# Seven products for eight in part of the first layer, with sums on GpSimd and copies on ScalarE

## The chip, the cores and the metric

The kernel runs on one core of a Trainium2 chip, with one launch. The metric is the device time of that core in microseconds (us), lower is better. Three runs of the kernel before took 331.85, 331.86 and 332.35 us; the median is 331.86 us. A separate execution was profiled, and its trace is what the views below are taken from. Its stated TensorE clock is 1.000 of full speed.

## The reference, cut to what matters

```python
B, H, S, Nb, D = 8, 8, 576, 16, 64           # q, k, v: B x H x S x D; beacon_k, beacon_v: B x H x Nb x D
scores = q @ concat(beacon_k, k).T / sqrt(D) # causal over k; the 16 beacon keys are seen by every query
a = softmax(scores)
x = (a @ concat(beacon_v, v)).transpose(0, 2, 1, 3).reshape(4608, 512)
h = x @ w_in                                 # first layer, 512 -> 2048
g = h * sigmoid(1.702 * h)
out = g @ w_out                              # second layer, 2048 -> 512, float32
```

So an attention over 8 batches is followed by two dense layers over 4608 tokens. All matrix products run on fp16 operands and add up in fp32.

## The kernel before, in words

**Attention.** The work is cut into 16 sets, a set being one batch and four of its heads. A set's scores are computed transposed (keys on the partitions) by `e_qk` (L458) in chunks of at most 512 columns for four heads, exponentiated by ScalarE in `e_exp` (L469), and masked by GpSimd in `e_mask` (L490). VectorE adds the key blocks of a set in `e_zadd` (L508). `e_av` (L545) forms the values and, with a matrix of ones, the row sums. VectorE turns and inverts the row sums (`e_z1`, `e_z2`) and writes the normalised values to `xT` (L580, `e_norm`). GpSimd also issues the loads of q, k, v and of the weights.

**The dense layers.** Tokens are taken in ten groups: two of 256 and eight of 512 (groups 2 to 9). The first layer of a group is 16 tiles of 128 hidden units each (`e_m1`, L604): four matmuls of 512 columns add up in one PSUM bank, and ScalarE applies the gate in `e_gelu` (L625) from PSUM to the fp16 tile `g`. The second layer of groups 2 to 9 is already done by Strassen's scheme in Winograd's form: `g` and `w_out` are cut into two by two blocks, VectorE makes four sums of blocks of `g` (`e_s`, L669), and TensorE does seven products instead of eight (`e_prod`, L718, 16 matmuls of 256 columns each). ScalarE copies the first product out of PSUM (`e_half`, L729), VectorE joins the others to it (`e_join`, L734), and SP stores the four quarters (`e_store4`, L741).

**PSUM.** The scores hold four banks. The four others form a ring (`RING`, `ring_tile`), shared by the tiles of the first layer, the values, and the products of the second layer. A ring bank is free again when its closing instructions (a gate, a norm, a join) are done.

**Order.** The order is written out beforehand: `Plan.run` takes operations with planned durations and dependences, and gives each engine a fixed sequence, which is then emitted. `choose` picks TensorE's next operation. `QUOTAS` says after how many chunks of scores a group's first layer may start, and when it has started (`inside`), its 16 tiles go before other dense work, and no scores are started. `T_ATT0` and `T_ATT1` spread the due times of the attention's loads and transposes. Each engine executes its sequence in order, so an instruction that waits holds up all that is behind it on its engine.

```python
        m1, m2 = first(("m1",)), first(("m2",))
        if m1 and inside:
            return m1
        if m1 and m2:
            return m2 if last == "m1" or free["ACT"] > t + 1500 else m1
```

TensorE's matmuls have three forms here: scores use row groups of 32, values use column groups of 32, and the dense layers use the whole array. In the order before, the form changes 145 times. After the last values, TensorE has the first layers of groups 8 and 9 and the products of groups 7, 8 and 9 left.

Of the kernel before, what the change touches and what calls it, by code (L numbers as in the profile page):

```python
# [13 lines left out]
NEAR = 500  # L14
IDLE = 800
# [9 lines left out]
class Plan:  # L25
# [5 lines left out]
    def __init__(self, ring):  # L31
        self.ops = []
        self.bank = [None] * ring
        self.tiles = {}
        self.closers = {}
        self.quota = {}
# [18 lines left out]
    def ring_free(self):  # L55
        best = None
        for i, key in enumerate(self.bank):
            t = 0
            for c in self.closers[key] if key is not None else ():
                t = None if t is None or c.start is None else max(t, c.end + 60)  # L60
            if t is not None and (best is None or t < best[0]):
                best = (t, i)
        return best

    def run(self):
# [8 lines left out]
        group, inside, ntile, nchunk = min(self.quota), False, 0, 0  # L74
        firsts = {}
        for o in self.ops:
            if o.kind == "m1":
                firsts.setdefault(o.pr, o)

# [5 lines left out]
        def allowed(o):  # L85
            if o.kind == "m2" and o.ring not in self.tiles:
                if sum(left_of[k] > 0 for k in self.tiles if k in left_of) >= 2:
                    return False
            if o.kind == "m1":
                return o.pr < group or (o.pr == group and (inside or group not in self.quota))  # L90
            if o.kind == "qk":
                return not inside
            if o.table is not None and o.table != table:
                return due_of_table[table] == 0
            return True
# [3 lines left out]
        while todo:  # L99
# [4 lines left out]
            slot = self.ring_free()  # L104
            ringt = slot[0] if slot else None
            for e, cand in avail.items():
                t = None
                for o in cand:
                    if not allowed(o):
                        continue  # L110
                    r = max(o.ready, o.due)
                    if o.ring is not None and o.ring not in self.tiles:
                        if ringt is None:
                            continue
                        r = max(r, ringt)
                    if t is None or r < t:
                        t = r
                if t is not None:
                    t = max(t, free[e])
                    if best is None or t < best[0]:  # L120
                        best = (t, e)
# [8 lines left out]
            for o in avail[e]:  # L130
# [3 lines left out]
                if o.ring is not None and o.ring not in self.tiles:  # L134
                    if ringt is None:
                        continue
                    r = max(r, ringt)
                if r <= t:
                    ok.append(o)
            if e == "PE":  # L140
                o = self.choose(ok, t, mode, last, free, inside)
# [8 lines left out]
            if e == "PE":  # L150
# [3 lines left out]
                if o.ring is not None and o.ring not in self.tiles:  # L154
                    self.tiles[o.ring] = slot[1]
                    self.bank[slot[1]] = o.ring
            if o.kind == "m1":
                ntile += 1 if o.pr == group else 0
                if inside and ntile == 16:
                    group, inside, ntile = group + 1, False, 0  # L160
# [30 lines left out]
    def choose(self, ok, t, mode, last, free, inside):  # L191
# [15 lines left out]
        late = first(("av",), lambda o: o.ready + 7000 <= t)  # L207
# [11 lines left out]
def kernel(  # L219
# [42 lines left out]
    pss = ctx.enter_context(tc.tile_pool(name="pss", bufs=1, space=bass.MemoryType.PSUM))  # L262
    psu = ctx.enter_context(tc.tile_pool(name="psu", bufs=1, space=bass.MemoryType.PSUM))

# [6 lines left out]
    QUOTAS = (19, 28, 38, 42, 48, 55, 55, 55)  # L271
    HM, HN = 256, NNT // 2
    xT = cst.tile([P, NKT, XR], F16, tag="xT", name="xT")
# [84 lines left out]
    plan = Plan(RING)  # L358

    def ring_tile(key):  # L360
        if key not in rings:
            i = plan.tiles[key]
            rings[key] = psu.tile([P, 512], F32, tag=f"u{i}", name=f"u{i}")
# [228 lines left out]

    def e_m1(g, n0, n1):
        t0, t1 = GROUPS[g]
        w = t1 - t0
        if g not in gts:
            gts[g] = gp.tile([P, NNT, 512], F16, tag="g", name="g")
# [90 lines left out]

    def quarter(g, i, j):
# [35 lines left out]

    def e_half(g, p, dst):
# [19 lines left out]
    T_ATT0, T_ATT1 = 17000, 249000  # L746
# [109 lines left out]

    def two_back(s, half):
# [3 lines left out]
    def values(s):  # L861
# [7 lines left out]
        for i in range(1, NJ if whole else 0):  # L869
# [3 lines left out]
                op("DVE", 75 + 0.517 * 4 * w, deps + sums[-1:], lambda i=i: e_zadd(s, i), pr=3, name="zadd")  # L873
            )
        for n, (x, half) in enumerate(order):
# [20 lines left out]
            if x == 2:  # L896
                z1 = op(
                    "DVE", 65 + 1.045 * cols, [avs[(s, x, half)]], lambda h=half: e_z1(s, h), pr=0, closes=key, name="z1"
# [4 lines left out]
                )  # L903
            else:
# [43 lines left out]
    SQ, SDVE, TDUE = 2, 0, 60000  # L948
# [9 lines left out]
    def products(g):  # L958
        eng = "POOL" if g < SDVE else "DVE"
        sd = {}  # L960
        for n0 in range(0, HN, SQ):
            n1 = n0 + SQ
            prev = []
            for i in range(4):
                deps = prev + done.get(g - 1, [])
                for n in range(n0, n1):
                    deps += [gates[(g, n)], gates[(g, n + HN)]]
# [8 lines left out]
        def prod(p):  # L976
            prev = []
            for n0 in range(0, HN, SQ):
# [3 lines left out]
                else:  # L982
                    deps += [gates[(g, n + (HN if p in (2, 4) else 0))] for n in range(n0, n0 + SQ)]
# [34 lines left out]
        store(c22, "u", 1, 1)  # L1018
        prod(3)
        c12 = join(3, "m", "m", [u4])  # L1020
        store(c12, "m", 0, 1)
        ends[g] = c12

    def mlp(g):
# [16 lines left out]
        for n0 in firsts:  # L1041
            n1 = n0 + n
            key = ("m1", g, n0)
# [56 lines left out]
    for o in done.get(NPL - 1, []) + done.get(NPL - 2, []) if tds else ():  # L1100
        also(tds[3], o)
    plan.quota.update(zip(range(GEL, NG), QUOTAS))
# [32 lines left out]
```

## Time and profile before

| | before |
|---|---|
| median of three runs | 331.86 us |
| profiled execution, its own time | 331.71 us |
| span of the profiled execution | 330.0 us |
| TensorE busy | 311.5 us |
| VectorE busy | 237.5 us |
| ScalarE busy | 203.6 us |
| GpSimd busy | 116.9 us |
| TensorE's first matmul starts at | 8.22 us |
| TensorE's last matmul ends at | 326.17 us |

The profiled execution is the time of one run; its span goes from the first to the last instruction, and 1.71 us of the run lie outside the span. Busy times count each instruction from its start to its end. Since TensorE works on several matmuls at once, the mean duration of one matmul in a group's row is longer than the step from one to the next; the step is read from the starts in the timeline. A line number in a view is a line of the kernel; "out<-in" gives the tiles written and read.

### The profile page before, as it was taken

The numbers are of one execution on the slowest core, as the hardware profiler recorded it, in microseconds if no ns is written. First come the engines' busy times: TensorE is split into PE (matmuls) and PEld (weight loads), VectorE is DVE, ScalarE is ACT, GpSimd is POOL, SyncE is SP. The second block draws the span as 40 slices with busy tenths as digits, with TensorE's granted clock in tenths as the row PEclk, the third lists the DMA queues.
The fourth block names the chain that finished last, engine by engine and source line by source line (L and its number), as shares of the span: only waits on it lengthen the run. The fifth ranks groups of instructions, "written<-read, shape, count | busy, mean of one in ns | idle before, by whom it ended". The sixth has DMA issues, their size and how long they took to land. (4 is left out here: it accounts for less than half of the span.)

```text
span 330.0 us, 9837 instructions
## 1 busy us (share of the span) xinstructions
PE 311.5 (94%) x4288; PEld 210.9 (64%) x4288; DVE 237.5 (72%) x478; ACT 203.6 (62%) x234; POOL 116.9 (35%) x178
## 2 busy tenths in 40 slices
PE   0699899999999999999999999999999999999995
PEld 0477666545885467646878877447774664746884
DVE  4847959796998788987999589978896630460484
ACT  1676487787767786777758586858677427175000
POOL 8765557572238205360427046702422000000000
PEclk9999999999999999999999999999999999999999
DMA  7999999569017903392149623930120000110122
GB/s 126 161 205 208 200 178 156 83 105 130 29 41 140 145 2 82 89 129 50 47 95 127 85 53 89 127 85 2 34 96 3 2 32 2 46 51 2 66 96 95
DMA packets 58219, 28.81 MB, mean 87 GB/s; under 512 B 41280, under 2 KB 53568, under 8 KB 58176
## 3 DMA queue, kind: packets, MB, share of 16 engines
q0 software_dynamic: 47552, 18.49, 47.7%
q1 hardware_dynamic: 10560, 9.69, 8.9%
q8 instruction: 33, 0.54, 0.7%
q14 instruction: 10, 0.08, 0.1%
q10 hardware_dynamic: 64, 0.01, 0.0%
HBM read 37.22 MB, written 9.44 MB: 141 GB/s over the span
## 5 line engine op out<-in xcount | busy, mean ns | idle before, releaser
L604 PE MATMUL u<-xT,w 128*128 128x512 f16 (+1 forms) x704 | 130.7, 343 | 2.1 <-DVE g L637 1.1
L469 ACT ACTIVATE E<-s 128x2048 f16<-128x2048 f32 (+4 forms) x66 | 98.8, 1514 | 42.7 <-PE s L458 42.0
L604 PEld LDWEIGHTS <-w 128*128 128x128 f16 x704 | 68.0, 98 | 58.5 <-issue 3.2
L625 ACT ACTIVATE g<-u 128x512 f16<-128x512 f32 x128 | 74.4, 598 | 43.2 <-PE u L604 43.0
L490 POOL TENSOR_SCALAR_AFFINE_SELECT E<-E 128x512 f16<-128x512 f16 (+3 forms) x78 | 52.0, 689 | 119.9 <-ACT E L469 116.2
L734 DVE SCALAR_TENSOR_TENSOR osb<-u,osb 128x512 f32<-128x512 f32 x56 | 37.4, 680 | 40.5 <-PE u L718 26.9
L718 PEld LDWEIGHTS <-g 128*128 128x128 f16 x512 | 48.6, 98 | 7.3 <-issue 0.2
L458 PE MATMUL s<-qT,kT 32*128 32x32 f16 (+20 forms) x1376 | 35.9, 235 | 11.7 <-DVE qT L429 10.3
L718 PE MATMUL u<-w,g 128*128 128x256 f16 x384 | 46.0, 273 | 0.0
L458 PEld LDWEIGHTS <-kT 32*128 32x128 f16 x1376 | 26.0, 95 | 29.1 <-issue 14.7
L718 PEld LDWEIGHTS <-sA 128*128 128x128 f16 x384 | 36.4, 98 | 4.9
L718 PE MATMUL u<-tB,sA 128*128 128x256 f16 x256 | 31.3, 273 | 0.0
L389 POOL DMA_DIRECT2D vb<-in_v_dram x32 | 27.3, 866 | 2.5 <-DMA kn<-in_k_dram 1.5
L545 PE MATMUL u<-E,vb 128*32 128x352 f16 (+8 forms) x928 | 27.7, 267 | 0.0
L580 DVE TENSOR_TENSOR xT<-u,rz 128x352 f16<-128x352 f32 (+2 forms) x52 | 24.9, 518 | 1.7 <-PE u L545 1.1
L508 DVE TENSOR_TENSOR zs<-zs,E 128x1344 f16<-128x1344 f16 (+2 forms) x36 | 23.5, 652 | 3.1 <-POOL E L490 0.5
L545 PEld LDWEIGHTS <-vb 128*32 128x32 f16 (+1 forms) x928 | 20.1, 98 | 5.4 <-issue 1.3
L429 DVE STREAM_TRANSPOSE kT<-kn 128x576 f32<-128x576 f32 x16 | 20.1, 1258 | 4.4 <-PE s L458 2.8
L669 DVE TENSOR_TENSOR sA<-g 128x512 f16<-128x512 f16 x32 | 12.8, 417 | 12.2 <-ACT g L625 11.9
L429 DVE STREAM_TRANSPOSE qT<-qn 128x576 f32<-128x576 f32 x16 | 20.0, 1249 | 2.2 <-PE s L458 1.8
L557 DVE STREAM_TRANSPOSE zt<-u 128x352 f32<-128x352 f32 (+2 forms) x32 | 13.8, 459 | 9.0 <-PE u L545 8.9
L718 PE MATMUL u<-tB,g 128*128 128x256 f16 x128 | 16.3, 273 | 0.0
(44 smaller groups left out, 229.1 us busy)
## 6 DMA issues: line engine op xcount, KB each, us to landing
out_dram<-osb SPq DMA_DIRECT2D x36, 256.0 KB, 2.2
kn<-in_k_dram POOLq DMA_DIRECT2D x16, 288.0 KB, 5.6
qn<-in_q_dram POOLq DMA_DIRECT2D x16, 288.0 KB, 6.3
vb<-in_v_dram POOLq DMA_DIRECT2D x24, 128.0 KB, 5.2
w<-in_moe_w_in_dram POOLq DMA_DIRECT2D x8, 256.0 KB, 9.2
w<-in_moe_w_out_dram POOLq DMA_DIRECT2D x4, 512.0 KB, 14.0
vb<-in_v_dram POOLq DMA_DIRECT2D x8, 112.0 KB, 3.7
vb<-in_v_dram POOLq DMA_DIRECT2D x8, 80.0 KB, 5.0
```

What stands on the lines that cost most here:

```text
L389: nc.gpsimd.dma_start(out=t[0 : hi - lo, j, h0:h1, :], in_=v[b, h0:h1, lo:hi, :].rearrange("h n d -> n h d"),)
L429: nc.vector.transpose(out=f32(dst.rearrange("p n e -> p (n e)")).rearrange("p (r t) -> p t r", t=TR), in_=f32(src[:, :]).rearrange("p (t c ...
L458: nc.tensor.matmul(sc[:, h, o : o + w], kT[s % NB2][r : r + 32, j * P : (j + 1) * P, d], qT[s % NB2][r : r + 32, a : a + w, d], start=(d = ...
L469: nc.scalar.activation(out=Es[s][:, :, c0:c1], in_=ss[i][:, :, o : o + c1 - c0], func=AFT.Exp, scale=0.125,)
L490: nc.gpsimd.affine_select(out=blk, in_=blk, compare_op=ALU.is_ge, fill=0.0, base=off + (Nb if j == 0 else 0), pattern=[[0, Q], [1, w]], ch ...
L508: nc.vector.tensor_tensor(out=t, in0=E[:, :, Z0:S] if i == 1 else t, in1=E[:, :, wcol[i] : wcol[i] + S - a], op=ALU.add,)
L545: nc.tensor.matmul(u[32 * h : 32 * h + 32, a:e], lhs, src[0:kw, h, col : col + e - a], start=first, stop=last,)
L580: nc.vector.tensor_tensor(out=xT[:, 2 * hs + x : 2 * hs + x + n, t0 : t0 + w], in0=rings[("av", s, x, half)][:, 0 : n * w].rearrange("p (n ...
L604: nc.tensor.matmul(u[:, o + a - t0 : o + e - t0], w1t[:, kp, nt * P : (nt + 1) * P], xT[:, kp, a % XR : (e - 1) % XR + 1], start=(kp == 0) ...
L625: nc.scalar.activation(out=gts[g][:, n0:n1, 0:w], in_=rings[("m1", g, n0)][:, 0 : n * w].rearrange("p (n w) -> p n w", n=n), func=AFT.Gelu ...
L718: nc.tensor.matmul(u[:, HM * mt : HM * (mt + 1)], lhs[:, n, mt * P : (mt + 1) * P], rhs[:, n, :], start=(n == 0 and mt == 0), stop=(n == H ...
L734: nc.vector.scalar_tensor_tensor(out=osbs[(g, dst)][:, :], in0=rings[("p", g, p)][:, :], scalar=scale_of(g), in1=osbs[(g, src)][:, :], op0 ...
```

## The change

The change works on the first layer of the last two groups. The 16 tiles of a group are four "quarters" of four tiles (two adjoining tiles and the two that stand eight further on). In two quarters of group 8 and three of group 9 the four tiles of 512 tokens are computed by Strassen's scheme instead of directly: `e_first` does seven products, each of four matmuls of 256 columns, in a PSUM bank of its own. VectorE makes four sums of blocks of `w_in` once (`e_wsum`) and four sums of blocks of `xT` per group (`e_xsum`). Products 1, 2, 3, 4 and 5 are copied from PSUM to SBUF in float32 by ScalarE (`e_fcopy`), products 6, 7 and 5 are added to such a copy by VectorE (`e_fjoin`), the four final sums are made by GpSimd in SBUF (`e_fadd`, float32, 128 x 512), and ScalarE's gate then reads SBUF (`e_fgelu`). These intermediates lie in the buffers of the attention's `E`, which are free by then.

The four PSUM banks of the scores become a second ring for these products once the last exponential is done. From group 8 on (`MIX`), tiles of the first layer no longer go before the products of the second layer. The last product of the last group is done for its two halves of rows in two banks, each with its own join and its own store, the second store from ScalarE's queue. Further, the constants of the plan are others (`NEAR`, `IDLE`, `QUOTAS`, `T_ATT0`, `T_ATT1`, `TDUE`, the planned time of `e_zadd`, the time after which values are preferred), so the order of the attention changes too. In the order after, TensorE's form changes 138 times.

```diff
--- before.py
+++ after.py
-NEAR = 500
-IDLE = 800
+NEAR = 680
+IDLE = 3300
+MIX = 8
+LATE1 = 0
...
-    def ring_free(self):
+    def ring_free(self, late):
         best = None
-        for i, key in enumerate(self.bank):
-            t = 0
+        if late and self.gate.start is None:
+            return None
+        for i in range(self.ring, self.ring + 4) if late else range(self.ring):
+            key = self.bank[i]
...
             if o.kind == "m1":
+                if group >= MIX:
+                    return True
                 return o.pr < group or (o.pr == group and (inside or group not in self.quota))
...
-                o = self.choose(ok, t, mode, last, free, inside)
+                o = self.choose(ok, t, mode, last, free, inside and (group < MIX or LATE1))
...
-        late = first(("av",), lambda o: o.ready + 7000 <= t)
+        late = first(("av",), lambda o: o.ready + 24000 <= t)
...
-    QUOTAS = (19, 28, 38, 42, 48, 55, 55, 55)
+    QUOTAS = (20, 28, 43, 46, 49, 55, 55, 55)
     HM, HN = 256, NNT // 2
+    FIRST = {7: (), 8: (1, 3, ), 9: (0, 1, 2, )}
+    FADD = 1150
...
     def ring_tile(key):
         if key not in rings:
             i = plan.tiles[key]
-            rings[key] = psu.tile([P, 512], F32, tag=f"u{i}", name=f"u{i}")
+            if i >= RING and not late_s:
+                scores.close()
+                late_s.append(ctx.enter_context(tc.tile_pool(name="psl", bufs=1, space=bass.MemoryType.PSUM)))
+            rings[key] = (psu if i < RING else late_s[0]).tile([P, 512], F32, tag=f"u{i}", name=f"u{i}")
         return rings[key]
...
+    def wsum(i):
+        t = late_tile(0)[:, 2048 * i : 2048 * (i + 1)] if i < 3 else late_tile(1)[:, 0:2048]
+        return t.rearrange("p (k n) -> p k n", k=2)
...
+    def e_wsum(i):
+        s1, s2, s4, s3 = (wsum(x) for x in range(4))
+        if i == 0:
+            add("DVE", s1, wq(1, 0), wq(1, 1), ALU.add)
...
+    def e_first(g, d, p):
+        u = ring_tile(("n", g, d, p))
+        lhs, rhs = {
+            1: (wq(0, 0), xq(g, 0, 0)),
+            2: (wq(0, 1), xq(g, 1, 0)),
+            3: (wsum(2), xq(g, 1, 1)),
+            4: (wq(1, 1), xsum(g, 2)),
+            5: (wsum(0), xsum(g, 0)),
+            6: (wsum(1), xsum(g, 1)),
+            7: (wsum(3), xsum(g, 3)),
+        }[p]
+        for t in range(2):
+            n = (2 * d + t) * P
+            for k in range(2):
+                nc.tensor.matmul(
+                    u[:, HM * t : HM * (t + 1)],
+                    lhs[:, k, n : n + P],
+                    rhs[:, k, :],
+                    start=(t == 0 and k == 0),
+                    stop=(t == 1 and k == 1),
+                )
+
+    def e_fcopy(g, d, p, dst):
+        nc.scalar.copy(out=part(d, dst), in_=rings[("n", g, d, p)][:, :])
+
+    def e_fjoin(g, d, p, src, dst):
+        nc.vector.tensor_tensor(
+            out=part(d, dst), in0=rings[("n", g, d, p)][:, :], in1=part(d, src), op=ALU.add
+        )
+
+    def e_fadd(d, src, dst):
+        nc.gpsimd.tensor_tensor(out=part(d, dst), in0=part(d, dst), in1=part(d, src), op=ALU.add)
+
+    def e_fgelu(g, d, x, i, j):
+        n0 = 2 * d + HN * i
+        nc.scalar.activation(
+            out=group_tile(g)[:, n0 : n0 + 2, HM * j : HM * (j + 1)],
+            in_=part(d, x).rearrange("p (t w) -> p t w", t=2),
+            func=AFT.Gelu_apprx_sigmoid,
+        )
 
...
+    def e_prod_last(g, mt):
+        u = ring_tile(("p", g, 3, mt))
+        for n in range(HN):
+            nc.tensor.matmul(
+                u[:, 0:HM],
+                sA[2][:, n, mt * P : (mt + 1) * P],
+                w2t[:, HN + n, HM:],
+                start=(n == 0),
+                stop=(n == HN - 1),
+            )
+
+    def e_join_last(g, mt):
+        t = osbs[(g, "m")][:, HM * mt : HM * (mt + 1)]
+        nc.vector.scalar_tensor_tensor(
+            out=t, in0=rings[("p", g, 3, mt)][:, 0:HM], scalar=scale_of(g), in1=t, op0=ALU.mult, op1=ALU.add
+        )
+
+    def e_store_last(g, mt):
+        t0 = GROUPS[g][0] + mt * P
+        (nc.scalar if mt else nc.sync).dma_start(
+            out=out[t0 : t0 + P, HM:], in_=osbs[(g, "m")][:, HM * mt : HM * (mt + 1)]
+        )
...
-    T_ATT0, T_ATT1 = 17000, 249000
+    T_ATT0, T_ATT1 = -1000, 245000
...
-                op("DVE", 75 + 0.517 * 4 * w, deps + sums[-1:], lambda i=i: e_zadd(s, i), pr=3, name="zadd")
+                op("DVE", 75 + 0.6 * 4 * w, deps + sums[-1:], lambda i=i: e_zadd(s, i), pr=3, name="zadd")
...
-    SQ, SDVE, TDUE = 2, 0, 60000
+    SQ, SDVE, TDUE = 2, 0, 75000
...
+        if g == NG - 1:
+            for mt in range(2):
+                o = op(
+                    "PE", HN * 109, [sd[(2, n0)] for n0 in range(0, HN, SQ)] + [last[5]],
+                    lambda mt=mt: e_prod_last(g, mt), kind="m2", pr=g,
+                    ring=("p", g, 3, mt), mode="m", name=f"m2.{g}.3.{mt}",
+                )
+                o = op(
+                    "DVE", 335, [o, u4], lambda mt=mt: e_join_last(g, mt), pr=2, closes=("p", g, 3, mt), name="join"
+                )
+                op("ACT" if mt else "SP", 60, [o], lambda mt=mt: e_store_last(g, mt), name="store")
+            return
...
+    def first_quarters(g, d, xs, old):
+        if not wsums:
+            for i in range(4):
+                wsums.append(op("DVE", 1130, wsums[-1:], lambda i=i: e_wsum(i), pr=3, name="wsum"))
+            needs.append((wsums[0], NSET - 3))
+            needs.append((wsums[3], NSET - 2))
+        if (g, 0) not in xsums:
+            deps = list(xs)
+            deps += [o for o in m1s.get(g - 1, []) if o.ring[0] == "n"]
+            for i in range(4):
+                xsums[(g, i)] = o = op("DVE", 336, deps, lambda i=i: e_xsum(g, i), pr=2, name="xsum")
+                deps = [o]
+            needs.append((xsums[(g, 0)], NSET - 2))
...
+        def prod(p):
+            deps = xs + old + [w for n in (2 * d, 2 * d + 1, 2 * d + HN) for w in w1_of[n]]
+            deps += [wsums[lhs[p]]] if lhs[p] is not None else []
+            deps += [xsums[(g, rhs[p])]] if rhs[p] is not None else []
+            last[p] = op(
+                "PE", 4 * 109, deps, lambda: e_first(g, d, p), kind="m1", pr=g,
+                ring=("n", g, d, p), mode="m", name=f"m1.{g}.{d}.{p}",
+            )
+            m1s.setdefault(g, []).append(last[p])
+
+        def buf(x):
+            return x.upper() if x in "uv" and d % 2 else x
+
+        def reads(x, o):
+            readers.setdefault(buf(x), []).append(o)
+
+        def writes(x):
+            return readers.pop(buf(x), [])
+
+        def copy(p, dst, closes=True):
+            o = op(
+                "ACT", 480, [last[p]] + writes(dst), lambda: e_fcopy(g, d, p, dst), pr=1,
+                closes=("n", g, d, p), name="fcopy",
+            )
+            needs.append((o, NSET - 1))
+            return o
+
+        def join(p, src, dst, deps):
+            return op(
+                "DVE", 605, [last[p]] + deps + (writes(dst) if src != dst else []),
+                lambda: e_fjoin(g, d, p, src, dst), pr=2, closes=("n", g, d, p), name="fjoin",
+            )
+
+        def final(src, dst, deps, i, j):
+            o = op("POOL", FADD, deps, lambda: e_fadd(d, src, dst), pr=3, name="fadd")
+            reads(src, o)
+            e = op("ACT", 520, [o] + old, lambda: e_fgelu(g, d, dst, i, j), pr=1, name="fgelu", table="g")
+            reads(dst, e)
+            for n in (2 * d + HN * i, 2 * d + HN * i + 1):
+                gates.setdefault((g, n), {})[j] = e
+
+        prod(1)
+        m = copy(1, "m")
+        prod(2)
+        final("m", "a", [m, copy(2, "a")], 0, 0)
+        prod(6)
+        u2 = join(6, "m", "v", [m])
+        reads("m", u2)
+        prod(7)
+        u3 = join(7, "v", "u", [u2])
+        prod(4)
+        final("u", "b", [u3, copy(4, "b")], 1, 0)
+        prod(5)
+        final("u", "c", [u3, copy(5, "c")], 1, 1)
+        u4 = join(5, "v", "v", [u3])
+        prod(3)
+        final("v", "a", [u4, copy(3, "a")], 0, 1)
...
+            if n0 % HN // SQ in FIRST.get(g, ()):
+                if n0 < HN and n0 % SQ == 0:
+                    first_quarters(g, n0 // SQ, xs, old)
+                continue
...
+    for o, s in needs:
+        for (t, x, h), d in avs.items():
+            if t == s:
+                also(o, d)
+        also(o, qks[CH_OF[NSET - 1][0]])
```

## The prediction

> **What bounds the kernel now.** I read the page's busy shares, its slices and the chain that ended last, then a table of stretches, then timelines for the step of each kind of work.
>
> ```profile
> PE 311.5 (94%) x4288; PEld 210.9 (64%) x4288; DVE 237.5 (72%) x478; ACT 203.6 (62%) x234; POOL 116.9 (35%) x178
> PE   0699899999999999999999999999999999999995
> PE u L604 16%; PE u L718 15%; PE u L545 2%; PE s L458 1%; DVE zs L508 1%; ACT E L469 1%; DVE osb L734 0%; ACT L625 0%; DVE xT L580 0%; ACT g L625 0%; DVEq L508 0%
> ```
>
> TensorE (PE) is idle for 18.5 us: 8.2 before its first matmul, 3.8 after its last, 2.1 at 9 us, and ten gaps of 0.1 to 1.1 us that add up to 4.3. The chain's end is dense matmuls alone. So work taken off PE counts one for one, unless it brings waits. In the table of stretches the second covers the time from the end of the last values to PE's end (columns: length, then PE, PEld, DVE, ACT, POOL busy):
>
> ```profile
> 17.60:267.80 250.20, 246.54 (x3724) 166.09 (x3713) 202.56 (x398) 176.72 (x194) 102.71 (x152) 1.00 0.64 93
> 267.80:326.20 58.40, 58.37 (x416) 39.84 (x408) 23.31 (x52) 20.30 (x34) 0.00 (x0) 1.00 0.12 42
> 326.20:330.00 3.80, 0.00 (x0) 0.00 (x0) 0.69 (x1) 0.00 (x0) 0.00 (x0) 1.00 0.39 138
> ```
>
> There PE is full, ScalarE a third busy, VectorE 40%, GpSimd idle: room for what the change adds. The timeline gives the steps (start, length, what):
>
> ```profile
> 287.74 13.98 PE L604 MATMUL u<-xT,w 128*128 128x512 f16 x64
> ...
> 301.55 3.66 PE L718 MATMUL u<-w,g 128*128 128x256 f16 x32
> ...
> 324.26 1.91 PE L718 MATMUL u<-w,sA 128*128 128x256 f16 x16
> ...
> 326.21 0.69 DVE L734 SCALAR_TENSOR_TENSOR osb<-u,osb 128x512 f32<-128x512 f32 x1 [0.46 <-PE u L718]
> ```
>
> From 287.74 to 301.55, 64 matmuls of 512 columns: 0.2158 us each. From 301.55 to 326.17, 224 of 256 columns: 24.44 us and 0.18 of pipeline, 0.1091 each.
>
> [...]
>
> ```profile
> 198.89 0.64 POOL L490 TENSOR_SCALAR_AFFINE_SELECT E<-E 128x512 f16<-128x512 f16 x1 [1.83 <-ACT E L469]
> 201.72 3.74 POOL L490 TENSOR_SCALAR_AFFINE_SELECT E<-E 128x512 f16<-128x512 f16 x4 [2.19 <-ACT E L469]
> ```
>
> Alone a mask takes 0.64. Four take at most 2.56, but 3.74 while VectorE ran two sums of two SBUF tensors (1.12 and 1.10 us): 1.2 us more for 2.2 of overlap, 0.55 per us.
>
> **The change part by part, against the profiled 331.71 (span 330.0 and 1.71 around).**
>
> *First layer.* Five quarters lose 5 x 16 matmuls of 512: 80 x 0.2158 = 17.27. They gain 5 x 7 x 4 of 256: 140 x 0.1091 = 15.27. PE: **-2.0**.
>
> *Changes of form.* The order has 138 instead of 145. Their price:
>
> ```profile
> 85.97 1.92 PE L718 MATMUL u<-tB,sA 128*128 128x256 f16 x16
> 87.82 0.65 PE L458 MATMUL s<-qT,kT 32*128 32x336 f16 x24
> 88.40 1.61 PE L545 MATMUL u<-E,vb 128*32 128x224 f16 x56
> ```
>
> 16 steps are 1.745 but the next work starts after 1.85: 0.11. The scores stream 4096 columns on four row groups, [...] and take 0.58: 0.15. So 7 x 0.13 = **-0.9**; bounds -1.1 and -0.5[...].
>
> *The end.* The last join covers 256 columns instead of 512. VectorE's rows rise by about 1.04 ns per column (514 at 352, 615 at 448, line L580), so 0.69 becomes 0.42: -0.27. The last store carries 128 KB instead of 256 (2.2 us to landing) from ScalarE's queue, whose instructions are done; smaller transfers are unshown on this queue, so 0 to -0.3, I take -0.1. The first half's join and store end within the second half's 8 x 0.109 = 0.87 of matmuls or shortly after. **-0.4**.
>
> *ScalarE, VectorE, GpSimd in the last 50 us.* ScalarE gets 25 copies; 20 gates go and 20 come, reading SBUF (at the same 0.6, by the nearest row). VectorE gets 15 joins of 0.69, eight sums of `xT` at 0.42 and four sums of weights at 1.2. GpSimd gets 20 adds[...]. Beside the adds VectorE runs group 8's 16 sums (step 0.336: four take 1.42), four sums of `xT` and one of weights, 7.9 us of some 34[...] I take 1.3. In group 9 a quarter's seven products alternate with as many steps of the second layer: 14 x 4 x 0.109 = 6.1 us. In that time GpSimd has 4 x 1.3 = 5.2, ScalarE nine instructions of 0.6 - 0.09: 4.6. Both fit, and that cover holds while an add stays under 6.1 / 4 = 1.53.
>
> New waits: ScalarE works in order, so a gate that waits for an add holds the copies behind it, these hold PSUM banks, and a product needs the bank of the fourth one before it. Following the first quarter of group 8 from the last values: product 1 ends after 4.3 us, its copy at 5.15, product 4 needs that bank at 6.1; product 3 needs a bank that a join frees at 6.7, and starts at 6.9. Group 8's sums for tiles 6 and 7 come through the second quarter's last add: there the slack is some 0.5 us. Taken: **+0.6** (0 to +3). Set 15's values now follow its row sums after only six steps of a product. From the start of set 14's values PE needs 1.55 for these, 0.37 for the row sums and 24 x 0.109 = 2.62 for the product, so it is there after 4.5 us. VectorE starts on the row sums at about 2.1 and has two turns (0.53, 0.37), two reciprocals (0.16, 0.18), two expansions (0.41, 0.55) and a norm (0.51) to do, 2.7 less what neighbours overlap: 4.5 to 5.0 with the signal. **+0.3** (0 to +1).
>
> *Attention in another order.* The three early sums of weights (3.6 us) fall among set 14's sums, where VectorE is over 90% busy in several slices; the first-layer tiles of groups 3 to 6 run in one piece. GpSimd's loads and masks keep their number, and their due times move earlier; SP's stores are 32 + 4 before, 31 + 4 + 1 and one on ScalarE after. The trace cannot price the reordering: the gaps total 4.3 now, so at best about -2; at worst I allow +3, three waits as long as the longest (1.09). **0** taken: PE's content there is the same, with the same three starts of a first layer right after scores (0.3 each).
>
> Sum: -2.0 - 0.9 - 0.4 + 0.6 + 0.3 = -2.4: 329.3 for the profiled execution. The median of the runs stands 0.15 above the profiled time: **329.5**.
>
> **Rivals.** (1) *The gain is spent on new gaps in the attention*: VectorE, 72% busy, is late for values and norms by some 2.4 us in all. For it: the DVE slices full of 9s. Against it: only 3.6 us of work is added there, over many operations. Time 331.9. (2) *GpSimd becomes the bound of the last stretch, and it ends slower.* At d us per add, group 9's 12 adds cost 12 (d - 1.53), group 8's about 1 us more; with the 0.6 of waits counted above taken off, the gain of 2.4 is gone from d = 1.7. At 1.9 it costs 5.4 - 0.6 = 4.8: 334.3. [...] Against it: [...] joins from PSUM read one SBUF tensor. (3) *The reordering also removes gaps*, about 1.5 of the 4.3: 328.0. That the change doesn't do what it says is excluded: the counts stand in the order.
>
> **How the numbers follow.** A measurement of this kernel can tell about 0.2%, 0.7 us, from no change. My forecast has 0.60 and rival 3 0.12: faster. Rival 1 has 0.13, of it 0.09 within 0.2% and 0.04 slower; rival 2 has 0.15. So 0.72 faster, 0.09 same, 0.19 slower. The range leaves out one in ten on each side: from 327.3, rival 3 with a better tail, to 333.0, most of rival 1 and rival 2 up to about d = 1.8.
>
> **What would show it.** PE's busy time near 309, its last stretch full, its last matmul near 324; the adds' row at 1.1 to 1.5 us; ScalarE's waits for GpSimd short; the last join near 0.42. Rival 2 shows as adds over 1.7 and PE gaps that ScalarE's copies end after the last values; rival 1 as gaps before 250 us, released by VectorE. I am wrong if PE's work falls by less than 2.5 us.

## The result, and the profile after

The changed kernel takes 340.51 us (median of four runs, 339.76 to 341.33) where the kernel before takes 331.86: a ratio of 1.0259, 95% interval 1.0239 to 1.0279. It is slower by some 8.7 us; the forecast was 329.5. The profiled execution took 339.76 us, with a span of 337.4 us where the one before had 330.0. Of the 8.05 us between these two executions 7.4 lie in the span; outside it the four runs differ by up to 0.6 us.

The page of the changed kernel: the busy shares, the slices of PE, VectorE and GpSimd, and the lines of the chain that ended last.

```profile
PE 310.4 (92%) x4348; PEld 216.4 (64%) x4348; DVE 261.2 (77%) x506; ACT 215.3 (64%) x259; POOL 144.2 (43%) x198
PE   0699899799999999999999999999999999869995
DVE  3847967498999679985899879978942986697693
POOL 8775585740339123900394047301430004476610
PE u L627 26%; PE u L831 21%; PE s L477 8%; PE u L564 7%; ACT E L488 4%; DVE sA L692 4%; PE u L672 3%; DVE osb L870 2%; DVE zs L527 2%; DMA bkf<-in_beacon_k_dram 2%; PE u L775 2%; DMA qn<-in_q_dram 2%; DVE E L787 1%; ACT g L648 1%; ACT L648 1%
```

PE's row has a 7 in its eighth slice (59 to 67 us), and an 8 and a 6 near 290 and 300 us, where before these slices read 9. The last two stand where GpSimd now has its adds. In the chain VectorE's sums (L692, `add`) have appeared, which were not in it before. So there are two places. In the table of stretches the second row runs from the first layer of group 8 to PE's end (length, then PE, PEld, DVE, ACT, POOL busy):

```profile
17.60:276.50 258.90, 252.17 (x3785) 171.74 (x3777) 206.80 (x405) 176.80 (x194) 103.87 (x152) 1.00 0.62 91
276.50:333.56 57.06, 51.83 (x420) 39.77 (x412) 43.10 (x73) 31.90 (x59) 26.26 (x20) 1.00 0.11 38
333.56:337.40 3.84, 0.00 (x1) 0.00 (x0) 0.42 (x1) 0.00 (x0) 0.00 (x0) 0.87 0.40 137
```

**The last stretch.** The kernel before needs 52.24 us for the work that remains at 276.50, by its own steps. Minus the 2.0 that the seven products save, 50.24 was due; it took 57.06, so 6.8 us are stalls: six PE gaps of 0.4 to 1.3 us (5.0 in all), about 0.16 behind each (a matmul's row there is 0.27 long, its step 0.11), and some 0.8 in seams too short to list. The timeline around two of them, rows of other instructions left out:

```profile
290.67 0.42 DVE L692 TENSOR_TENSOR g<-g 128x512 f16<-128x512 f16 x1
290.74 1.47 POOL L792 TENSOR_TENSOR E<-E 128x512 f32<-128x512 f32 x1 [2.79 <-ACT E L784]
291.01 1.49 DVE L692 TENSOR_TENSOR sA<-g,sA 128x512 f16<-128x512 f16 x1
...
292.42 0.68 DVE L787 TENSOR_TENSOR E<-u,E 128x512 f32<-128x512 f32 x1
...
293.15 0.60 PE L775 MATMUL u<-xT,E 128*128 128x256 f16 x4 [0.98 <-DVE E L787]
...
297.52 1.48 DVE L692 TENSOR_TENSOR E<-xT 128x512 f16<-128x512 f16 x1
...
299.06 0.61 PE L775 MATMUL u<-E 128*128 128x256 f16 x4 [1.28 <-DVE E L692]
```

The sum that starts at 290.67 takes VectorE its usual 0.42 us. The next, of the same shape, starts while GpSimd's add runs and takes 1.49: it ends 0.29 after the add has ended. A join (L787) queues behind it, and a product needs the bank which that join frees: 0.98 us of PE. At 297.52 the same happens to a sum of `xT` blocks, and the product that reads it waits 1.28. GpSimd's adds are the ones hardly slowed: 1.47 beside the sum at 291.01, 1.27 where they meet none. The answer for one line gives least, median and longest duration in ns, then the first and last start:

```profile
L792 POOL TENSOR_TENSOR E<-E x20: 1266/1275/1473, 282.2 to 320.4; 128x512 f32<-128x512 f32 x20
L692 DVE TENSOR_TENSOR g<-g x32: 407/418/1486, 75.6 to 326.8; 128x512 f16<-128x512 f16 x32
L692 DVE TENSOR_TENSOR E<-xT x4: 405/515/1483, 277.7 to 297.5; 128x512 f16<-128x512 f16 x4
```

In the whole last stretch 14 of VectorE's sums overlap an add. Ten of them are lengthened, by 8.1 us in all, and every one of the ten ends 0.28 or 0.29 us after an add has ended. So these ten did not run more slowly beside an add, they stood still until it was over. The 15 joins with one input in PSUM that overlap an add keep 0.68 to 0.69.

**The attention.** PE's gaps between 14 and 276 us are 7.3 us in all, where they were 4.3. The largest new one is here (timeline):

```profile
65.18 0.66 PE L477 MATMUL s<-qT,kT 32*128 32x336 f16 x24 [0.15 <-ACT E L488]
65.91 1.88 ACT L488 ACTIVATE E<-s 128x2048 f16<-128x2048 f32 x1 [0.25 <-PE s L477]
67.84 0.64 PE L477 MATMUL s<-qT,kT 32*128 32x384 f16 x24 [2.00 <-ACT E L488]
68.42 3.63 PE L627 MATMUL u<-xT,w 128*128 128x512 f16 x16
```

Two chunks of scores stand next to each other. There is one score tile, so the second chunk waits until the exponential has emptied it, 1.88 us. Before, the first layer of group 2 came between them, since its quota was 19 chunks and not 20 (read from the plan; the quota was not changed by itself). Two more new ones, 0.30 and 0.72 us, stand at 142 and 144 us.

The span's 7.4 us are then: start +0.2, gaps of the attention +3.1, fewer changes of form about -0.7 (the remainder up to 276.50), first layer -2.0, stalls of the last stretch +6.8, tail 0.

### The profile page after: what moved, and what is told of

It is laid out like the page before. It is cut to its first block, busy times and chain, and to the rows that moved or that the text cites. A ratio compares the mean times of both kernels' runs of the same rounds, so it can differ in the third digit from the quotient of the medians.

```text
span 337.4 us, 10059 instructions
## 1 busy us (share of the span) xinstructions
PE 310.4 (92%) x4348; PEld 216.4 (64%) x4348; DVE 261.2 (77%) x506; ACT 215.3 (64%) x259; POOL 144.2 (43%) x198
## 4 chain that ended last, share of the span: by engine, by line
PE 67%; DVE 17%; ACT 8%; DMA 3%; issue 3%; POOL 1%; SPq 0%; DVEq 0%; ACTq 0%; POOLq 0%
PE u L627 26%; PE u L831 21%; PE s L477 8%; PE u L564 7%; ACT E L488 4%; DVE sA L692 4%; PE u L672 3%; DVE osb L870 2%; DVE zs L527 2%; DMA bkf<-in_beacon_k_dram 2%; PE u L775 2%; DMA qn<-in_q_dram 2%; DVE E L787 1%; ACT g L648 1%; ACT L648 1%
## 5 line engine op out<-in xcount | busy, mean ns | idle before, releaser
L627 PE MATMUL u<-xT,w 128*128 128x512 f16 (+1 forms) x624 | 113.8, 337 | 3.5 <-ACT g L648 1.2
L509 POOL TENSOR_SCALAR_AFFINE_SELECT E<-E 128x512 f16<-128x512 f16 (+3 forms) x78 | 53.1, 708 | 114.7 <-ACT E L488 112.8
L627 PEld LDWEIGHTS <-w 128*128 128x128 f16 x624 | 60.2, 98 | 50.2 <-issue 5.5
L648 ACT ACTIVATE g<-u 128x512 f16<-128x512 f32 x108 | 62.9, 599 | 36.7 <-PE u L627 36.5
L870 DVE SCALAR_TENSOR_TENSOR osb<-u,osb 128x512 f32<-128x512 f32 x55 | 36.6, 678 | 19.8 <-PE u L831 18.5
L831 PE MATMUL u<-w,g 128*128 128x256 f16 x384 | 47.9, 273 | 0.2
L792 POOL TENSOR_TENSOR E<-E 128x512 f32<-128x512 f32 x20 | 26.3, 1330 | 47.1 <-ACT E L784 42.0
L831 PEld LDWEIGHTS <-sA 128*128 128x128 f16 x368 | 34.8, 98 | 7.8 <-DVE sA L692 2.2
L831 PE MATMUL u<-tB,sA 128*128 128x256 f16 x256 | 33.5, 273 | 1.7 <-DVE sA L692 1.6
L692 DVE TENSOR_TENSOR sA<-g 128x512 f16<-128x512 f16 x32 | 15.2, 489 | 12.5 <-ACT g L648 8.2
```

The costliest lines, as they stand in the source:

```text
L509: nc.gpsimd.affine_select(out=blk, in_=blk, compare_op=ALU.is_ge, fill=0.0, base=off + (Nb if j == 0 else 0), pattern=[[0, Q], [1, w]], ch ...
L627: nc.tensor.matmul(u[:, o + a - t0 : o + e - t0], w1t[:, kp, nt * P : (nt + 1) * P], xT[:, kp, a % XR : (e - 1) % XR + 1], start=(kp == 0) ...
L648: nc.scalar.activation(out=gts[g][:, n0:n1, 0:w], in_=rings[("m1", g, n0)][:, 0 : n * w].rearrange("p (n w) -> p n w", n=n), func=AFT.Gelu ...
L692: (nc.vector if eng == "DVE" else nc.gpsimd).tensor_tensor(out=out, in0=a, in1=b, op=op)
L831: nc.tensor.matmul(u[:, HM * mt : HM * (mt + 1)], lhs[:, n, mt * P : (mt + 1) * P], rhs[:, n, :], start=(n == 0 and mt == 0), stop=(n == H ...
L870: nc.vector.scalar_tensor_tensor(out=osbs[(g, dst)][:, :], in0=rings[("p", g, p)][:, :], scalar=scale_of(g), in1=osbs[(g, src)][:, :], op0 ...
```

## The experiments

Each was compared with runs of the kernel before on its own chip, whose medians were 331.63 to 331.86 us.

### Without the final sums (no_final_sums)

```diff
-        nc.gpsimd.tensor_tensor(out=part(d, dst), in0=part(d, dst), in1=part(d, src), op=ALU.add)
+        pass
```

> The changed kernel without GpSimd's 20 final sums: the gates read a part that lacks the second summand, all else keeps its order. Theory 1 (GpSimd's float32 adds hold VectorE's sums of two SBUF tensors, VectorE falls behind, and TensorE waits for it) and theory 2 (ScalarE's gates wait for the adds' results and hold the copies behind them): of the 6.8 us that TensorE loses in the last stretch at most 1.5 stay, about 334.5 us. Theory 3 (the copies, joins and banks of the seven products are too slow by themselves): 339 us or more.

Measured: 334.67 us (334.18 to 335.3), ratio 1.0089 (1.0073 to 1.0104), so 5.8 us below the changed kernel (5.6, if each is taken against the kernel before on its own chip). VectorE's sums, same lines of the same answer as above:

```profile
L692 DVE TENSOR_TENSOR g<-g x32: 411/418/852, 75.8 to 321.6; 128x512 f16<-128x512 f16 x32
L692 DVE TENSOR_TENSOR E<-xT x4: 403/416/418, 278.9 to 296.5; 128x512 f16<-128x512 f16 x4
```

The longest, 0.85, stands in the attention, beside one of GpSimd's masks; after 281 us none is longer than 0.43. VectorE's busy time falls from 261.2 to 253.7 us with the same 506 instructions. One PE gap of 0.73 us and one of 0.14 are left in the last stretch, which takes 51.59 us (277.71 to 329.30) instead of 57.06: 1.3 us of stalls are left of 6.8. So the adds cost 5.5 us there and about that in the median. This does not yet tell whether the kernel waited for their results or was held by their running.

### The same sums, not awaited (sums_not_awaited)

GpSimd does the same adds, into a buffer that nobody reads, so no gate waits for them; the gates read the sum without its last term.

```diff
-        nc.gpsimd.tensor_tensor(out=part(d, dst), in0=part(d, dst), in1=part(d, src), op=ALU.add)
+        nc.gpsimd.tensor_tensor(out=f32(qn[0][:, 0:1024]), in0=part(d, dst), in1=part(d, src), op=ALU.add)
```

> The changed kernel with the 20 adds at the same places and sizes, but written to a buffer that nobody reads, so no gate waits for one; the gates read a part that lacks the second summand. Theory 1[...]: nearly the changed kernel's time, 339 to 340.5 us, with single sums of VectorE still up to 1.5 us. Theory 2 (waits for the adds' results): like the kernel without the adds, about 335 us.

Measured: 338.75 us (338.39 to 340.8), ratio 1.0223 (1.0192 to 1.0254). With no gate waiting for an add (a copy of ScalarE into a buffer that an add reads still comes after it in the plan), the sums on VectorE still look like this:

```profile
L692 DVE TENSOR_TENSOR sA<-sA,g x32: 410/424/1490, 75.1 to 324.0; 128x512 f16<-128x512 f16 x32
L692 DVE TENSOR_TENSOR g<-g x32: 407/417/1487, 75.9 to 326.0; 128x512 f16<-128x512 f16 x32
```

and the last stretch keeps 4.0 of its 5.0 us of gaps and takes 56.06 us (276.67 to 332.73). By the medians about 1.8 us (340.51 - 338.75) is waiting for the adds and some 4 (338.75 - 334.67) is VectorE held while they run. By the last stretches of the three traces, each at full clock there, it is 1.0 (57.06 - 56.06) and 4.5 (56.06 - 51.59). The runs of the changed kernel spread over 1.6 us and those of this one over 2.4, so the split is rough; which part is the larger is not in doubt.

### The plan's constants alone (constants_only)

The new code with all three edits to the work switched off: direct first layers, no mixing, the last product whole. What is left against the kernel before are the constants, the planned time of `e_zadd` and one dependence that the changed plan adds: `e_z1` of a set's row sums waits for the reciprocal two steps back. These were not taken apart.

```diff
-    FIRST = {7: (), 8: (1, 3, ), 9: (0, 1, 2, )}
+    FIRST = {}
-MIX = 8
+MIX = 99
-        if g == NG - 1:
+        if g == NG:
```

> The kernel before with the changed plan's constants alone (NEAR, IDLE, QUOTAS, T_ATT0, T_ATT1, TDUE, planned sums, late values); no Strassen in the first layer, last product whole. If the attention's new order costs what the two traces show (3.1 us more gaps and 0.2 at the start, less 0.7 for fewer changes of form): 334.5 us, with a gap of 2.0 us of TensorE before the second of two neighbouring scores near 66 us. If the order of the attention is neutral and the last stretch took all: 331 to 332 us.

Measured: 334.92 us (334.45 to 335.43), ratio 1.0098 (1.0081 to 1.0115): +3.3 us. Its gaps in the attention are 7.7 us, with the one of 2.00 at 66 us.

The runs of this kernel, of the changed one and of `no_final_sums` spread more than others, and their mean granted clock is 0.993 to 0.995 in some runs and 0.999 to 1.0 in others. The table of stretches of `no_final_sums`, whose mean is 0.993, shows where (the number after POOL's is the clock):

```profile
66.00:68.00 2.00, 0.02 (x4) 0.02 (x5) 0.00 (x0) 1.88 (x1) 2.00 (x4) 1.00 2.13 141
68.00:70.00 2.00, 2.00 (x30) 1.10 (x30) 1.87 (x3) 1.31 (x2) 2.00 (x3) 0.85 1.80 228
70.00:72.00 2.00, 2.00 (x7) 0.63 (x5) 2.00 (x2) 1.97 (x3) 1.65 (x4) 0.50 1.07 188
72.00:74.00 2.00, 2.00 (x9) 0.87 (x8) 1.76 (x4) 1.71 (x4) 0.00 (x0) 0.79 0.41 79
```

PE stands still for 2.0 us, from 65.98 to 67.98, and some time after that the clock is halved in this execution: by the three rows for (0.15 + 0.50 + 0.21) x 2 / 0.50 = 3.4 us. In the profile of the changed kernel it stays at 1.00 at the same place. The runs of `no_final_sums` with the lower mean took 334.92 and 335.3 us, the others 334.43 and 334.18: about 0.8 us. In this trace a rest of 2.0 us, with 0.66 us of scores ahead of it and 0.64 behind it, came before the fall; how long a rest it takes was not shown.

### The score tile freed earlier (early_release)

`constants_only`, but of the exponential of chunk 18 only 64 columns come from the scores; the rest is filled from a tile of weights at the same cost to ScalarE. The score tile is free earlier, nothing else is changed.

```diff
+        if i == 18:
+            r = c1 - c0 - 64
+            nc.scalar.activation(out=Es[s][:, :, c0 : c0 + 64], in_=ss[i][:, :, o : o + 64], func=AFT.Exp, scale=0.125)
+            nc.scalar.activation(out=Es[s][:, :, c0 + 64 : c1], in_=w1t[:, 0, 0 : 4 * r]..., func=AFT.Exp, scale=0.125)
+            return
```

> The kernel before with the changed plan's constants (as in the run with the constants alone), but of the one exponential between the two neighbouring scores near 66 us only 64 of 448 columns per head come from the scores; the rest is filled from a weight tile at the same cost to ScalarE. So the scores' PSUM is free some 1.5 us earlier and nothing else changes. If TensorE's 2.0 us gap there costs its length and makes the clock drop in some executions: 333.0 to 333.4 us, gap under 0.6 us, granted clock 0.998 or more in every run. If ScalarE's pace sets the time there anyway: 334.9 us.

Measured: 333.9 us (333.48 to 334.06), ratio 1.0055 (1.0041 to 1.0069), 1.0 us below `constants_only` (1.2 by the differences from the kernel before on each chip), at a clock of 0.998 to 1.0 in every run. The time lies between the two forecasts. The gap falls from 2.00 to 0.51, but the next one, where the first layer waits for ScalarE's gates, grows from 0.40 to 1.12: ScalarE has the same work, and part of the wait moves one place on. So the wait for the tile is the cause of the 2.0 us and, as far as four runs tell, of the drops of the clock, and ScalarE bounds what its removal can give. The other gaps (0.30 and 0.72 around 144 us, before the first layer of group 4) stay.

### The constants of before under the new work (old_constants)

```diff
-NEAR = 680
-IDLE = 3300
+NEAR = 500
+IDLE = 800
-    QUOTAS = (20, 28, 43, 46, 49, 55, 55, 55)
+    QUOTAS = (19, 28, 38, 42, 48, 55, 55, 55)
...
```

> The changed kernel with the constants of the plan before, so that the attention's order is the one before up to set 14; first layer by Strassen and last product by halves as in the changed kernel. If the constants cost 2.6 us: 337.9 us, and the first 245 us of the trace agree with the kernel before. If the constants are neutral: 340.5 us.

Measured: 338.17 us (338.05 to 338.46), ratio 1.0194 (1.0179 to 1.021). The order is that of before up to set 14, and its form changes 145 times again. The gap at 66 us is 0.39 again; the last stretch has the same six gaps, 5.0 us in all. So the constants and the new work each cost by themselves: +3.3 and +6.5 against before, 9.8 together where both at once cost 8.7. Where the 1.1 between these goes was not followed.

### The last product by halves alone (halves_only)

The constants of before, `FIRST` empty, `MIX` at 99, and the added dependence of `e_z1` taken out again.

> The kernel before with its last product by halves of its rows and nothing else. The forecast's term: -0.4 us, 331.2 to 331.3 us. The rival from the trace of the changed kernel (last join ends 0.24 us earlier against TensorE's end, the last store from ScalarE's queue ends the run 0.24 us later against its issue): no change, 331.6 us.

Measured: 331.91 us, ratio 1.0001 (0.9993 to 1.0009). Nothing is gained.

### The final sums on VectorE (vector_finals, vector_finals_4)

The constants of before. A final sum is a join that reads its product in PSUM, so GpSimd has no add, and only product 1 of a quarter is copied by ScalarE. The second kernel has four quarters instead of five.

```diff
-            o = op("POOL", FADD, deps, lambda: e_fadd(d, src, dst), pr=3, name="fadd")
+            o = op("DVE", 605, [last[p]] + deps + writes(dst), lambda: e_fjoin(g, d, p, src, dst),
+                   pr=2, closes=("n", g, d, p), name="fjoin")
```

> As the changed kernel with the constants before, but the 20 final sums are made by VectorE straight from PSUM (a join of 0.69 us instead of a copy on ScalarE and an add on GpSimd), so GpSimd is idle in the last stretch. Theory 1 (GpSimd's adds held VectorE): no sum of VectorE above 0.45 us there, TensorE idle 2.5 us at most in the last stretch, about 332 us in spite of 20 more joins on VectorE. If VectorE's load is the limit[...]: 335 us or more.

> The same with four quarters (two of group 8, two of group 9) instead of five. TensorE has 4 x 0.43 = 1.7 us less work than before and VectorE 12 us more. Theory 1: 331.0 to 332 us. If VectorE's load is the limit: 1 to 2 us below the run with five quarters.

Measured: 332.24 us, ratio 1.001 (1.0001 to 1.0018), and 331.57 us, ratio 0.999 (0.9982 to 0.9998). Taking the adds off GpSimd gives back 5.9 us (338.17 - 332.24) of what `old_constants` costs, though VectorE has 20 operations more; 20 of ScalarE's copies go with the adds. No sum of 128 x 512 is longer than 0.70, and that one stands at 84 us beside a mask; the six gaps are gone. With five quarters a PE gap of 0.85 is left, with four none.

Four quarters should have brought 4 x 0.40 = 1.6 us, and brought 0.3. In the last stretch the 1.6 is there: from 274.75 to PE's end at 325.96 are 51.21 us, by the steps 64 x 0.2158 + 340 x 0.1091 + 0.18 = 51.09. The rest was lost ahead of that: this work would have begun at 273.48 in the kernel before, 1.27 us earlier. Up to the first layer at 213 us it is 0.17 later, then come three new PE gaps of 0.15, 0.36 and 0.16 at 243 to 254 us, and some 0.4 that no view lists. The order differs from that of before just from set 14 on, where VectorE makes the sums of weights.

### The sums of weights after the last values (vector_finals_late, vector_finals_late_8, gpsimd_finals_late)

All three have the constants of before. The first has final sums on VectorE, three quarters, all in group 9, and TensorE's order of before until the products of group 9 begin. The second has a fourth quarter, in group 8. The third is the first with the final sums on GpSimd.

```diff
-            needs.append((wsums[0], NSET - 3))
+            needs.append((wsums[0], NSET - 1))
-    FIRST = {7: (), 8: (1, 3, ), 9: (0, 1, 2, )}
+    FIRST = {8: (), 9: (0, 1, 2)}
-MIX = 8
+MIX = 9
```

> The constants of before, final sums on VectorE from PSUM, only quarters 0, 1 and 2 of group 9, and the sums of weights made after the last values instead of between the last three sets; the mixing of first and second layer starts with group 9. TensorE's order is then that of before up to the last values and the first layer of group 8. Theory: each quarter takes 16 x 0.2158 - 28 x 0.1091 = 0.40 us off TensorE and it was the disturbed order around sets 14 and 15 (three new gaps of 0.67 us in all, and about 0.4 more) that took it back in the two runs with final sums on VectorE. So -1.2 here: about 330.7. Rival: alternating short pieces of four matmuls have a cost of their own that eats the 0.40 of a quarter; then 331.8, the same as before.

> As vector_finals_late, with one quarter of group 8 as well (quarter 3) and the mixing from group 8 on, so four quarters. Theory: -1.6, about 330.3, unless the sums of weights (four of 1.2 us, now after the last values) come too late for group 8's products, which would show as TensorE gaps ended by VectorE's sums near 280 us. Rival: 331.8.

> As vector_finals_late, with the final sums on GpSimd as in the changed kernel (12 adds in SBUF, and ScalarE's copies of products 2 to 5 that they need). TensorE has the same work. Theory (the adds hold VectorE's two-input sums[...]): sums of up to 1.5 us again, TensorE gaps of some 2 to 3 us behind them in group 9, so 332.7 to 333.7, about 2 to 3 us above vector_finals_late. Rival (the adds cost only together with group 8's sums of weights and of xT at the disturbed end of the attention): 330.7 to 331.2.

Measured:

| | us | ratio, interval | PE from the first layer at 213 us to its end |
|---|---|---|---|
| before | 331.83 | | 113.27 |
| vector_finals_late | 331.01 | 0.9974 (0.9966 to 0.9983) | 112.08 |
| vector_finals_late_8 | 331.59 | 0.9995 (0.9987 to 1.0003) | 112.11 |
| gpsimd_finals_late | 333.18 | 1.0044 (1.0031 to 1.0056) | 114.25 |

The first one is faster than both kernels, by 0.26% than the one before. Its last part is 1.19 us shorter, the 3 x 0.40 of the theory, with no gap in it; of this 0.8 reaches the median. In its profile PE's first matmul starts at 8.86 us where it was 8.22 before; why that start lies between 8.4 and 9.0 in the new kernels was not followed. That short alternating pieces have a price of their own is refuted for these three quarters.

The second was expected at 330.3 and missed, and not by TensorE gaps near 280 us, which its forecast named: VectorE, with 11 instructions more than in the first, is itself late at the end. A gap of 0.17 waits for its sum, and its last joins come in a row and end 1.5 us after PE (timeline):

```profile
323.16 1.98 PE L842 MATMUL u<-w,sA 128*128 128x256 f16 x16
323.36 2.61 DVE L870 SCALAR_TENSOR_TENSOR osb<-u,osb 128x512 f32<-128x512 f32 x4 [1.06 <-PE u L831]
...
325.89 0.74 DVE L852 SCALAR_TENSOR_TENSOR osb<-u,osb 128x256 f32<-128x256 f32 x2
```

The third costs 2.2 us more than the first for 12 adds moved to GpSimd, within the theory's range, but not by the theory's way, in which PE waits for VectorE's sums. It has two PE gaps, both behind a copy of ScalarE (timeline and waits; the columns of the waits are total, times, longest):

```profile
290.62 2.50 DVE L692 TENSOR_TENSOR sA<-sA,g 128x512 f16<-128x512 f16 x4
290.65 1.51 POOL L792 TENSOR_TENSOR E<-E 128x512 f32<-128x512 f32 x1 [40.34 <-ACT E L784]
...
295.58 1.42 DVE L692 TENSOR_TENSOR g<-g 128x512 f16<-128x512 f16 x4
295.80 2.33 POOL L792 TENSOR_TENSOR E<-E 128x512 f32<-128x512 f32 x1 [3.64 <-DVE E L787]
```

```profile
L792 POOL TENSOR_TENSOR E<-E x12: 1265/1273/2325, 290.6 to 312.3; 128x512 f32<-128x512 f32 x12
```

```profile
ACT g L796 <- POOL E L792: 7.4, 8, 2.3
PE u L775 <- ACT E L784: 1.6, 2, 0.9
```

At 290.62 four sums take 2.50 instead of 1.42 beside the add. But at 295.80 an add starts 0.22 us after a run of four sums on VectorE that keep their 1.42, and it takes 2.33. So here GpSimd is the one that waits, the gates wait for it, and the copies stand behind the gates, at the first of the two PE gaps. Ahead of the second, three adds of usual length come in a row and the gates wait for these too. The hold goes both ways; what decides it was not settled: both adds start during one of several sums in a row, and the first got in after one of them, the second only when all were done.

## Why the prediction was wrong, by its own steps

- **New waits of the last stretch: +0.6 (0 to +3) was the step that failed; 6.8 was measured.** The price of an add, 1.3 us, was the author's estimate, since the trace of before has no such add. It came out near that, 1.33 us on the mean: 1.27 or 1.28 where it meets no sum, at most 1.47 where it meets one in this kernel. The error was who pays where the two overlap. From four masks that stretched beside two sums, the prediction charged GpSimd alone, 0.55 us per us of overlap, and left VectorE's sums at 0.42. In the runs a sum of two SBUF tensors that meets an add takes up to 1.49. The trace of before had this already, in VectorE's sums of key blocks:

```profile
L508 DVE TENSOR_TENSOR zs<-E x12: 1104/1112/1580, 68.7 to 246.3; 128x1856 f16<-128x1856 f16 x12
156.42 0.63 POOL L490 TENSOR_SCALAR_AFFINE_SELECT E<-E 128x512 f16<-128x512 f16 x1 [10.67 <-ACT E L469]
156.44 1.58 DVE L508 TENSOR_TENSOR zs<-E 128x1856 f16<-128x1856 f16 x1 [0.40 <-ACT E L469]
```

Seven of these twelve meet no mask and take 1.10 to 1.13 us; of the five that do, three take 1.34 to 1.58. Even in the prediction's own example VectorE paid: its second sum, 1.10 us, has 1344 columns, and such a sum takes 0.85 to 0.86 where no mask runs. The test of 1.53 to 1.7 us per add was therefore the wrong one: at 1.33 the loss was already there. Rival 2 had the right two engines and the right sign, 334.3, but looked for slow adds (the longest of the 20 is 1.47). A standstill, not a slower pace, is what these traces show for such sums (0.42 becomes 1.49).
- **Copies behind gates that wait for an add** were named, and are real: 1.0 to 1.8 us of the 5.8 (`sums_not_awaited`), and most of the 2.2 in `gpsimd_finals_late` by its waits. There the copies stand behind gates that wait for adds, the first of which itself waits for VectorE. For ScalarE's step the prediction took 0.6 - 0.09 = 0.51, the author's estimate; in the trace of before gates of 0.59 to 0.63 that stand next to each other start 0.48 to 0.50 apart.
- **The attention in another order: 0 (-2 to +3) was sized wrongly; +3.1 us of gaps.** "The same three starts of a first layer right after scores" looked at the starts, and not at two chunks of scores in a row, which the new quota of 20 puts there. With one score tile the price was in the trace before: an exponential of 128 x 2048 took 1.88 us there too. That the clock would also fall after such a gap, to 0.50 in the trace of `no_final_sums`, was not foreseen; the median of the changed kernel stands 0.75 above its profiled time, and such a drop is the likely reason (not shown: only its profiled execution has a trace).
- **First layer -2.0: right.** The last stretches of the kernels with final sums on VectorE follow the two steps within 0.2 us, once their gaps are counted, and three quarters gave 1.19. PE's busy time fell by only 1.1, to 310.4 and not to 309, since a matmul's row of 0.27 us counts as busy and the step is 0.11, so that each of the six gaps leaves some 0.16 in the busy time; the sign that the prediction named was a poor one.
- **Changes of form -0.9: about right.** Some -0.7 by the remainder in the changed kernel, and in `constants_only` (139 changes) PE ends 2.9 later for 3.9 of later start and gaps: -1.0. The 0.15 at the scores sets their 0.58 against an estimate of 0.43, by the two steps of the trace of before: 0.2158 - 0.1091 = 0.1067 for 256 columns, four times that for 1024.
- **The end -0.4: nothing.** The last join is 0.42 as said, and it ends 0.46 after PE instead of 0.73. But from the issue of the last store to the end of the span are 3.4 us instead of 3.1, and `halves_only` is at 1.0001. What the join gives goes between the issue of that smaller store, on ScalarE's queue, and the end; whether its size or its queue does it was not tried.
- **Set 15's values +0.3: not seen** as a gap; the changed kernel has none of PE between 230 and 286 us.

The range's upper end, 333.0, failed since both bounds of +3 were treated as unlikely together, and the bound on the new waits was too narrow by itself.

## What to carry to other kernels

In this kernel work put on an idle GpSimd was paid for by VectorE too, where VectorE added two SBUF tensors: a sum of 0.42 us took up to 1.49 beside an add, and one of 1.10 up to 1.58 beside a mask, which has one input. Price such work as time in which VectorE's sums can stand still, and ask who waits for these. Here the same sums were cheaper on VectorE, straight from PSUM (332.24 us against 338.17), though VectorE was the busier engine (77% busy to GpSimd's 43% in the changed kernel): fewer copies, no held sums. When a planner's constants change together with the work, look in the new order for neighbours that share one buffer, and run the constants alone. Extra work should go where it doesn't reorder a part that is already full.

## What was not expected of the hardware

- A float32 add of 128 x 512 on GpSimd and VectorE's fp16 sum of two SBUF tensors hold each other up: the sum goes from 0.42 to as much as 1.49 us while the add stays at 1.27 to 1.47, or the add goes from 1.27 to 2.33 while four sums keep their 1.42. A lengthened sum ends 0.28 or 0.29 us after an add has ended. The 15 joins with one input in PSUM that overlap an add keep 0.68 to 0.69.
- After a rest of 2.0 us TensorE's clock fell to half for 3.4 us in one traced execution (`no_final_sums`) and stayed full in others with the same rest (the changed kernel, `constants_only`); with 0.51 us in its place the clock was at least 0.998 in all four runs.
